# One Strassen level in the first product of an FFN beside a long convolution, PSUM seeded by ScalarE, and a second product in two-bank tiles

## The chip, the cores and the metric

The kernel runs on one core of one Trainium2 chip. The time is the device time of one execution in microseconds (us), the median over runs. The engines are named as in the profile: PE is the matrix engine, PEld its weight loads, DVE the vector engine, ACT the scalar engine, POOL the GpSimd engine, SP the queue that starts most DMAs.

## What is computed

The input x is 2048 tokens by 576 channels. After a layer norm two branches are added to x: a gated long convolution and a feed-forward network (FFN) with hidden width 4608.

```python
xn = layernorm(x)
# branch A: short conv over k, times v, long causal conv through an FFT, times xn
kv = shortconv(k, shift_k) * v
y  = irfft(rfft(kv, 2S) * rfft(ssm_k, 2S))[:S] + kv * ssm_D
a  = xn * y
# branch B
b  = relu(xn @ w1) @ w2          # w1 576x4608, w2 4608x576
return x + a + b
```

All arrays are float32. To keep that precision on PE, each operand is split into a high part and a low part (ACT copies the high part in a rounded format, DVE or POOL subtracts it from the source), and a product a·b is made of three matmuls: high·high, high·low, low·high.

## The kernel before

**The FFN.** The 4608 hidden columns are worked through in 12 chunks of 384 (`FT` = 3 tiles of 128), twice: the first pass for token blocks 0 and 1, the second for blocks 2 and 3 (512 tokens each). One turn is a chunk and a block. In it `mm1` makes three hidden tiles of 128 columns by 512 tokens: 14 matmuls of 512 columns each (L414: four chunks of 128 channels, three matmuls each, and the last 64 channels, where high and low part share one tile, with two). ACT writes relu of the result (`hh`, L420), DVE the rest (`ll`, L421). `mm2` multiplies the hidden tiles of the turn before with w2: for each of 4 tiles of 128 tokens and each half of 288 channels nine matmuls (L439), and DVE adds the result to the sum in SBUF (`acc`, L443, L449). PSUM has two banks for `mm1`, three for `mm2` and three for the convolution.

**The weights.** Each chunk's w1 and w2 are loaded raw by DMAs that POOL starts, ACT copies the high parts (L379, L388), and POOL subtracts (`split_lo`, L348). POOL reads two SBUF operands in each of these.

**The convolution** is a generator, `conv`, with four stages in this order: the filter's first transform (L474 to L482), the short convolution, gate and first transform of the data (L567 to L576, `tap`, `gate`, `stack`), the product in the frequency domain (L638 to L703), and the inverse transform with the output (L763 to L833). `tick` is called after every few matmuls of the FFN with their cost in PE columns. It lets the generator make at most one step at each call, and only while a balance that grows with the cost is not negative. So the convolution's instructions lie between those of the FFN in one fixed program order, and on each engine all of them run in that order. A step that waits holds up what stands behind it on its engine.

**The layer norm.** For the first block the rows are only centred before they are turned; the factor 1/std is applied where DVE adds `mm2`'s result (L443, one three-operand instruction). The other blocks are normalized beforehand.

Of the kernel before, what the change touches and what calls it, by code (L numbers as in the profile page):

```python
# [26 lines left out]
FT = 3  # L27
FC = FT * P
NCHUNK = DFF // FC
# [4 lines left out]
HT = T // HALVES  # L34

# [6 lines left out]
WARM_TILE = (0, 4, 0, 0)  # L42
LATE = (0, 1, 5)


W_MM1 = 14 * 512
W_MM2 = FT * 6 * NH
PAUSE = 16000
START = 4000
PAUSES = 17  # L50
# [9 lines left out]
FFT_TOTAL = N_FK * W_FK + N_FX * W_FX + N_FM * W_FM + N_FO * W_FO  # L60

SPLITS = {(0, 1): ((1, 0),), (0, 2): ((1, 1),), (1, 0): ((1, 2), (2, 0)), (1, 1): ((2, 1),),
          (1, 2): ((2, 2),)}
SPLITS0 = {(1, 0): ((1, 0), (1, 1)), (1, 1): ((1, 2), (2, 0)), (1, 2): ((2, 1), (2, 2))}
FFN_TOTAL = NCHUNK * NB * (FT * W_MM1 + BT * W_MM2)

# [46 lines left out]
def h3_ffn_kernel(ctx: ExitStack, tc, x, k, v, shift_k, ssm_k, ssm_D, w1, w2, fwd, inv, mid, out):  # L113
# [7 lines left out]
    wp = ctx.enter_context(tc.tile_pool(name="wp", bufs=2))  # L121
    hp = ctx.enter_context(tc.tile_pool(name="hp", bufs=2 * FT))
    xp = ctx.enter_context(tc.tile_pool(name="xp", bufs=2))
# [15 lines left out]
    rows_n = dram.tile([HB, BT // 2, 2, P, D], F32, name="rows_n")  # L139

# [33 lines left out]
    def load_x(t, tag, bufs, **queues):  # L174
        pair = xp.tile([P, 2, D], F32, tag=tag, name=f"{tag}{t}", bufs=bufs)
        move(pair, x, slice(t, t + 2), **queues)
        return pair

    def acc_pair(t, pair):
        pairs[t] = pair  # L180
        acc[t], acc[t + 1] = pair[:, 0, :], pair[:, 1, :]

    def load_acc(t, **queues):
        acc_pair(t, load_x(t, "acc", HT // 2, **queues))

    def add_x(t):

        for u in range(U):
            nc.gpsimd.dma_start(pairs[t][halves(u)[0]], x[u, :, t:t + 2], accum_op=OP.add)

    def stats(t, src):
        st = xp.tile([P, 2, 6], F32, tag="bn", name=f"bn{t}", bufs=4)
        for h in range(2):
            nc.vector.bn_stats(st[:, h, :], src[:, h * NH:(h + 1) * NH])
        nc.vector.bn_aggr(mv[:, t, :], st)

    def inv_std(t0, n):

        q = xp.tile([P, 3, 2 * BT], F32, tag="q", name=f"q{t0}")[:, :, :n]
# [8 lines left out]
    def normalized(dst, src, t):  # L208
        nc.vector.tensor_scalar(dst, src, mv[:, t, 0:1], rstd[:, t:t + 1],
                                op0=OP.subtract, op1=OP.mult)  # L210

    xT = {}
    done = {}

    def xT_tiles(b):
        hi = xp.tile([P, 4, 512], F32R, tag="xhi", name=f"xhi{b}")
        lo = xp.tile([P, 4, 512], F32R, tag="xlo", name=f"xlo{b}")
        hl = xp.tile([P, 512], F32R, tag="xhl", name=f"xhl{b}")
        xT[b] = (hi, lo, hl)

    def split_x(b, c, ps, cols=slice(0, 512)):
        hi, lo, hl = xT[b]
        if c < 4:
            high = nc.scalar.activation(hi[:, c, cols], ps[:, cols], AF.Copy)
            low = nc.vector.tensor_tensor(lo[:, c, cols], ps[:, cols], hi[:, c, cols],  # L225
                                          OP.subtract)
        else:
            high = done["act"] = nc.scalar.activation(hl[:64, cols], ps[:64, cols], AF.Copy)
            low = nc.vector.tensor_tensor(hl[64:, cols], ps[:64, cols], hl[:64, cols],
                                          OP.subtract)  # L230
        return high, low

    def centre(dst, src, t, how, behind=None):

        if how != "dve":
            neg = xp.tile([P, BT], F32, tag="neg", name=f"neg{t}", bufs=4)[:, :1]
        with tc.issue_after(behind.ins) if behind else nullcontext():
            if how == "act":  # L240
                nc.scalar.activation(dst, src, AF.Copy, scale=-1.0 / D, accum_out=neg)
            else:
                stats(t, src)
                if how == "dve":
                    return nc.vector.tensor_scalar(dst, src, mv[:, t, 0:1], None,
                                                   op0=OP.subtract)
                last = nc.vector.tensor_scalar(neg, mv[:, t, 0:1], -1.0, None, op0=OP.mult)
            act = nc.scalar.activation(dst, src, AF.Identity, bias=neg)
        return act if how == "act" else last

    def row_pairs(t0):
        pairs = [xp.tile([P, 2, D], F32, tag="xn", name=f"xn{t}", bufs=BT // 2)
                 for t in range(t0, t0 + BT, 2)]
        return [pairs[i // 2][:, i % 2, :] for i in range(BT)]
# [6 lines left out]
    def first_xT(srcs):  # L261

        xT_tiles(0)
        ps = []
        for c in range(5):
            ps.append(ps_o.tile([P, 512], F32, tag="o", name=f"psx{c}") if c >= 3 else fft_psum())
# [710 lines left out]
```

## Time and profile before

| | |
|---|---|
| median of 3 runs | 1071.23 us (1068.26 to 1071.31) |
| span of the profiled execution, first to last instruction | 1064.9 us |
| PE busy | 1055.7 us, 99% |
| PEld, DVE, ACT, POOL busy | 950.8, 747.9, 539.7, 408.8 us |
| granted PE clock | 1.00 in every 50 us but the last, 0.96 |
| the chain that ended last | PE 93%, DVE 5%, DMA 1% |

The profiled execution has no time of its own beside its span. The span is 6.3 us below the median of the runs. In a row of instructions the columns are: line, engine, operation, output <- inputs with their shapes, count | busy us, mean ns of one | idle time of the engine just before them and what ended it. A row of the timeline begins with its start and its duration. A row of the windows gives, for a stretch of the span, its length, and then PE, PEld, DVE, ACT and POOL busy in us, with the number of instructions; then the clock, the DMA share and GB/s.

### The profile page before, as it was taken

To read this page: it belongs to the slowest core of one execution; us is meant where nothing else is said; L and a number is where in the kernel's file an instruction comes from. 1 tells how busy PE (TensorE), PEld (TensorE's weight loads), DVE (VectorE), ACT (ScalarE), POOL (GpSimd) and SP (SyncE) were. 2 spreads that over 40 slices of the span, in tenths; PEclk is the share of its full clock that TensorE was granted. 3 is DMA by queue.
4 is the path that set the end of the run, shared out by engine and by line. 5 is a ranking of instruction groups with operands and counts; after the bars stand their busy time and mean duration, and the time that the engine had idled before them with its cause. 6 is when DMAs were issued, how large, how long until landed. Compare 5 with 4: busy or idle time off the path is not lost.

```text
span 1064.9 us, 17284 instructions
## 1 busy us (share of the span) xinstructions
PE 1055.7 (99%) x6228; PEld 950.8 (89%) x6228; DVE 747.9 (70%) x1207; ACT 539.7 (51%) x967; POOL 408.8 (38%) x465
## 2 busy tenths in 40 slices
PE   9999999999999999999999999999999999999998
PEld 6889999999998998999988888888888899999998
DVE  5322787858999788986557677766667737776774
ACT  5321787822433423424367777767776635443430
POOL 5261352423514424324425263424243364545520
PEclk9999999999999999999999999999999999999999
DMA  9990555674644448535566798667585679758624
GB/s 209 188 215 1 147 146 186 186 190 131 188 120 152 123 147 242 130 113 150 173 174 179 186 258 230 209 153 218 138 236 136 156 188 262 196 128 203 155 77 111
DMA packets 136785, 179.18 MB, mean 168 GB/s; under 512 B 69037, under 2 KB 73359, under 8 KB 136700
## 3 DMA queue, kind: packets, MB, share of 16 engines
q1 hardware_dynamic: 109756, 109.39, 38.5%
q0 software_dynamic: 26624, 67.95, 25.3%
q8 instruction: 49, 0.80, 0.3%
q10 hardware_dynamic: 320, 0.74, 0.3%
q14 instruction: 36, 0.29, 0.1%
HBM read 121.40 MB, written 42.47 MB: 154 GB/s over the span
## 4 chain that ended last, share of the span: by engine, by line
PE 93%; DVE 5%; DMA 1%; issue 0%; ACT 0%; SPq 0%
PE psh L414 41%; PE pso L439 41%; PE psf L647 6%; PE psf L481 3%; DVE e L570 1%; DVE c L571 1%; PE psf L830 1%; PE psf L831 1%; PE psf L700 1%; DVE xs L475 1%; DMA acc<-in_x 1%; DVE acc L443 0%; DVE c L567 0%; DVE acc L449 0%; DVE ll L421 0%
## 5 line engine op out<-in xcount | busy, mean ns | idle before, releaser
L348 POOL TENSOR_TENSOR l<-r,h 128x640 fp32r<-128x640 f32 (+1 forms) x144 | 229.7, 1613 | 316.8 <-ACT h L379 226.0
L439 PE MATMUL pso<-l,hh 128*128 128x288 f32 x1152 | 338.3, 295 | 0.0
L439 PE MATMUL pso<-h,hh 128*128 128x288 f32 x1152 | 336.2, 295 | 2.0 <-DVE acc L443 1.8
L439 PE MATMUL pso<-h,ll 128*128 128x288 f32 x1152 | 337.8, 295 | 0.0
L414 PE MATMUL psh<-xlo,h 128*128 128x512 f32 x576 | 226.4, 393 | 0.2 <-DVE xlo L225 0.2
L414 PE MATMUL psh<-xhi,h 128*128 128x512 f32 x576 | 225.5, 392 | 1.0 <-DVE ll L421 0.8
L439 PEld LDWEIGHTS pso<-h,hh 128*128 128x128 f32 x1152 | 215.3, 188 | 11.1 <-DVE acc L443 2.6
L414 PE MATMUL psh<-xhi,l 128*128 128x512 f32 x576 | 224.8, 391 | 0.0
L439 PEld LDWEIGHTS pso<-l,hh 128*128 128x128 f32 x1152 | 216.1, 188 | 7.6
L439 PEld LDWEIGHTS pso<-h,ll 128*128 128x128 f32 x1152 | 215.8, 188 | 1.7
L420 ACT ACTIVATE hh<-psh 128x512 fp32r<-128x512 f32 x144 | 85.6, 595 | 207.6 <-PE psh L414 204.8
L421 DVE SCALAR_TENSOR_TENSOR ll<-psh,hh 128x512 fp32r<-128x512 f32 x144 | 98.8, 687 | 110.2 <-ACT hh L420 109.4
L449 DVE TENSOR_TENSOR acc<-pso,acc 128x288 f32<-128x288 f32 x272 | 121.5, 451 | 63.3 <-PE pso L439 60.2
L414 PEld LDWEIGHTS psh<-xhi,l 128*128 128x128 f32 x576 | 108.2, 188 | 21.0
L414 PEld LDWEIGHTS psh<-xhi,h 128*128 128x128 f32 x576 | 108.1, 188 | 19.1 <-DVE ll L421 1.0
L414 PEld LDWEIGHTS psh<-xlo,h 128*128 128x128 f32 x576 | 108.1, 188 | 17.5 <-DVE xlo L225 0.8
L683 POOL DMA_DIRECT2D st<-yl x72 | 36.1, 533 | 106.6 <-PE psf L647 41.2
L443 DVE SCALAR_TENSOR_TENSOR acc<-pso,rstd,acc 128x288 f32<-128x288 f32 x96 | 48.1, 512 | 27.1 <-PE pso L439 26.5
L388 ACT ACTIVATE h<-r 128x576 fp32r<-128x576 f32 x72 | 48.4, 678 | 24.4 <-issue 13.2
L475 DVE TENSOR_TENSOR ks<-kt,ks 64x288 fp32r<-64x288 f32 x64 | 57.9, 905 | 3.9 <-ACT ks L474 1.9
L414 PE MATMUL psh<-xhl,h 128*128 128x512 f32 x144 | 56.3, 391 | 0.0
L414 PE MATMUL psh<-xhl,l 128*128 128x512 f32 x144 | 56.1, 390 | 0.0
(121 smaller groups left out, 1472.7 us busy)
## 6 DMA issues: line engine op xcount, KB each, us to landing
r<-in_w POOLq DMA_DIRECT2D x69, 288.0 KB, 5.5
r<-in_w POOLq DMA_DIRECT2D x23, 768.0 KB, 6.2
zk<-zk SPq DMA_DIRECT2D x32, 288.0 KB, 2.7
zx<-zx SPq DMA_DIRECT2D x32, 288.0 KB, 2.9
ztk<-zk SPq DMA_DIRECT2D x36, 256.0 KB, 4.0
ztx<-zx SPq DMA_DIRECT2D x36, 256.0 KB, 3.8
k<-k SPq DMA_DIRECT2D x72, 128.0 KB, 2.8
zo<-zy SPq DMA_DIRECT2D x32, 288.0 KB, 4.5
```

Of the source, the lines that this page charges most:

```text
L348: return nc.gpsimd.tensor_tensor(dst, src, hi, OP.subtract)
L388: nc.scalar.activation(h2, r2, AF.Copy)
L414: last = nc.tensor.matmul(ps, a, m, start=i == 0, stop=i == len(seq) - 1)
L420: done["act"] = nc.scalar.activation(hh, ps, AF.Relu)
L421: lows.append(nc.vector.scalar_tensor_tensor(ll, ps, 0.0, hh, op0=OP.max, op1=OP.subtract))
L439: nc.tensor.matmul(ps[:, :NH], a[:, cols], m[:, dc], start=n == 0, stop=n == 3 * FT - 1)
L443: done["acc"] = nc.vector.scalar_tensor_tensor(acc[t][:, dc], ps[:, :NH], rstd[:, t:t + 1], acc[t][:, dc], op0=OP.mult, op1=OP.add)
L449: done["acc"] = nc.vector.tensor_tensor(acc[t][:, dc], ps[:, :NH], acc[t][:, dc], OP.add)
L475: nc.vector.tensor_tensor(dst[other], src[own], dst[own], OP.subtract)
L481: nc.tensor.matmul(ps[:, :NH], w[:, u, n, :], stk, start=n == 0, stop=n == 1)
L647: nc.tensor.matmul(ps, a, m, start=n == 0, stop=n == 2)
L683: nc.gpsimd.dma_start(st[q * A2:(q + 1) * A2, i % GR, :], yl[i * A2:(i + 1) * A2, :])
```

## The change

The chunks become 256 columns wide (`FT` = 2), 18 for each half of the tokens. A chunk with two token blocks is a "quad", 36 in all. In a quad the four hidden tiles (2 of columns, 2 of tokens) times the four channel chunks form a two by two block product. Before it took eight products of 6 matmuls; now `quad` makes seven, by Strassen's scheme in Winograd's form, from sums of w1 blocks and of x blocks. The last 64 channels stay as they were (`rest`, 8 matmuls). Quad 0 is still made in the old way (`classical`). Everything else of the first product follows from that:

- The sums of w1 are made by POOL (`sums`, four more instructions per quad) and are split too, so that POOL splits 14 blocks of 128 by 128 per quad, and the last rows, where 256 columns had 8.
- The sums of x are made once by DVE; those of the second half are made during the first stage of the generator (`later_operands`, new), written to DRAM and loaded back when they are needed.
- The partial products are carried on in PSUM. ACT copies one bank to the next with the sign turned (`c`, `d`), or to SBUF (`u2`, `p5`), and DVE adds two of them.
- The second product has one tile of two banks (2 times 288 channels) per 128 tokens, two such tiles, and one DVE addition for both halves. Two of eight such units in a quad are "seeded": ACT copies the sum so far into PSUM, PE adds to it, and ACT copies it back, without DVE.
- PE's order in a quad is written out: a product, a unit of the second product (12 matmuls of 288 columns), a product, and so on. The convolution has two banks for three.
- `tick` is called 26 times per quad, with 1024, 1536 or 3456 columns. Before it was 14 times per turn, with 2592 or 3584. `START` and `PAUSES` differ.
- The first block is now normalized fully before it is turned, and 1/std is no longer applied later.

The diff, cut to its core:

```diff
-FT = 3
+FT = 2
-NCHUNK = DFF // FC
+NQ = DFF // FC
+QUADS = HALVES * NQ
-WARM_TILE = (0, 4, 0, 0)
+WARM_TILE = (0, 10, 0, 4)
+SEEDED = (1, 5)
-START = 4000
-PAUSES = 17
+START = 40000
+PAUSES = 19
-    ps_h = ctx.enter_context(tc.tile_pool(name="ps_h", bufs=2, space=PSUM))
-    ps_o = ctx.enter_context(tc.tile_pool(name="ps_o", bufs=3, space=PSUM))
-    ps_f = ctx.enter_context(tc.tile_pool(name="ps_f", bufs=3, space=PSUM))
+    ps_h = ctx.enter_context(tc.tile_pool(name="ps_h", bufs=1, space=PSUM))
+    ps_o = ctx.enter_context(tc.tile_pool(name="ps_o", bufs=2, space=PSUM))
+    ps_f = ctx.enter_context(tc.tile_pool(name="ps_f", bufs=2, space=PSUM))
...
+    def normalize_pair(xn, t):
+        for i in range(2):
+            stats(t + i, acc[t + i])
+        inv_std(t, 2)
+        normalized(xn[t % BT], acc[t], t)
+        return normalized_act(xn[t % BT + 1], acc[t + 1], t + 1)
...
+    def sums(g):
+        r1 = raw1[g]
+        t = sums_w[g] = wp.tile([P, 4, 2, P], F32, tag="sums", name=f"sums{g}")
+        w00, w01 = r1[:, 0:2, :P], r1[:, 0:2, P:]
+        w10, w11 = r1[:, 2:4, :P], r1[:, 2:4, P:]
+        for to, a, b in ((3, w00, w01), (0, t[:, 3], w11), (2, t[:, 0], w10), (1, w11, w01)):
+            nc.gpsimd.tensor_tensor(t[:, to], a, b, OP.add)
...
+    def product(ps, w, off, o, start=False):
+        for c in range(2):
+            h, l = w[:, 0, off + c, :], w[:, 1, off + c, :]
+            hi, lo = xo[o][:, 0, c, :], xo[o][:, 1, c, :]
+            matmuls(ps, ((h, hi), (h, lo), (l, hi)), start and c == 0)
+            tick(3 * W_MM)
...
+    def quad(g, units):
...
+        product(b, wa[g], 0, "00", start=True)
+        nc.scalar.activation(c, b, AF.Copy, scale=-1.0)
+        split_w2(g, 0)
+        unit(0)
+        product(b, wa[g], 2, "01")
+        rest(b, g, b0, 0)
+        hidden(g, 0, 0, b)
+        if more:
+            load_w2(g + 1, 0)
+            sums(g + 1)
+            split_a(g + 1)
+        unit(1)
+        product(c, wb[g], 0, "s2")
+        nc.scalar.activation(u2, c, AF.Copy)
+        split_w2(g, 1)
+        unit(2)
+        product(c, wb[g], 2, "s3")
+        nc.scalar.activation(d, c, AF.Copy, scale=-1.0)
+        if more:
+            split_b(g + 1)
+        unit(3)
+        product(d, wc[g], 0, "11")
+        rest(d, g, b1, 0)
+        hidden(g, 1, 0, d)
+        unit(4)
+        rest(c, g, b1, 1)
+        unit(5)
+        product(e, wc[g], 2, "s1", start=True)
+        nc.scalar.activation(p5, e, AF.Copy)
+        nc.vector.tensor_tensor(c, c, p5, OP.add)
+        hidden(g, 1, 1, c)
+        if more:
+            split_c(g + 1)
+        unit(6)
+        rest(e, g, b0, 1)
+        product(e, wd[g], 0, "s4")
+        nc.vector.tensor_tensor(e, e, u2, OP.add)
+        hidden(g, 0, 1, e)
+        if more:
+            split_d(g + 1)
+            split_r(g + 1)
+            if g + 2 < QUADS:
+                load_w1(g + 2)
+        unit(7)
...
+    def open_unit(g, b, i, n):
+        t = token(g, b, i)
+        ps = open_ps[g, t] = ps_o.tile([P, 2, 512], F32, tag="o", name=f"pso{g}_{t}")
+        if n in SEEDED and 0 < g < QUADS - 1:
+            seeded.add(t)
+            nc.scalar.activation(ps[:, :, :NH], two(acc[t]), AF.Copy)
...
+        if t in seeded:
+            done["act"] = nc.scalar.activation(two(acc[t]), ps[:, :, :NH], AF.Copy)
+            seeded.remove(t)
+        else:
+            done["acc"] = nc.vector.tensor_tensor(two(acc[t]), ps[:, :, :NH], two(acc[t]), OP.add)
+        tick(W_UNIT)
```

How the instructions move is shown at three places. The first is DVE in the short convolution, as one pass through four taps of a token tile. Before (`c`, `e`, `xs` are the convolution's sum, product and split; `acc` the second product's sum, `ll` a hidden tile's low part):

```order
L443 SCALAR_TENSOR_TENSOR acc_93<-pso_0_0_3084,rstd,acc_93 128x288
L443 SCALAR_TENSOR_TENSOR acc_93<-pso_0_1_3098,rstd,acc_93 128x288
L567 TENSOR_TENSOR c_3138<-k_3066,sk 128x576
L570 TENSOR_TENSOR e_1_3153<-k_2934,sk 128x576
L475 TENSOR_TENSOR xs_0_3095<-c_2992,xs_0_3095 64x576
L475 TENSOR_TENSOR xs_1_3113<-c_2992,xs_1_3113 64x576
L571 TENSOR_TENSOR c_3138<-c_3138,e_1_3153 128x576
L421 SCALAR_TENSOR_TENSOR ll_1_1_3157<-psh_1_1_3130,hh_1_1_3156 128x512
```

And now, in quad 13:

```order
L733 TENSOR_TENSOR e_1_3973<-k_3724,sk 128x576
L614 TENSOR_TENSOR acc_114<-pso_6_4262,acc_114 128x576
L734 TENSOR_TENSOR c_3932<-c_3932,e_1_3973 128x576
L634 TENSOR_TENSOR xs_0_3891<-c_3772,xs_0_3891 64x576
L634 TENSOR_TENSOR xs_1_3926<-c_3772,xs_1_3926 64x576
L733 TENSOR_TENSOR e_2_4005<-k_3595,sk 128x576
L614 TENSOR_TENSOR acc_114<-pso_7_4294,acc_114 128x576
L730 TENSOR_TENSOR c_4110<-k_4042,sk 128x576
L734 TENSOR_TENSOR c_3932<-c_3932,e_2_4005 128x576
L733 TENSOR_TENSOR e_3_4014<-k_3229,sk 128x576
L472 SCALAR_TENSOR_TENSOR ll_1_0_4362<-psh_4_4325,hh_1_0_4361 128x512
```

Of these eleven rows eight are the convolution's, of the eight before it was five; an `acc` row now covers both halves of the channels.

The second is POOL in the same stage. Before (`l` is a low part, `r` a raw weight, `wx` a transform matrix):

```order
L348 TENSOR_TENSOR l_7_0_2949<-r_7_2669,h_7_0_2948 128x640
L348 TENSOR_TENSOR l_7_1_3044<-r_7_2669,h_7_1_3043 128x640
L468 DMA wx_2940<-in_fwd 128x512
L348 TENSOR_TENSOR l_6_2_2815<-r_6_2_2413,h_6_2_2814 128x576
L370 DMA r_7_2_2818<-in_w 128x576
L348 TENSOR_TENSOR l_7_2_3117<-r_7_2669,h_7_2_3116 128x640
L348 TENSOR_TENSOR l_7_0_3125<-r_7_0_2677,h_7_0_3124 128x576
```

And now (`wa`, `wc`, `wd`, `wr`, `w` are the low parts of the blocks of w1 and of w2):

```order
L403 TENSOR_TENSOR wc_4122<-sums_3945,wc_4122 128x512
L627 DMA wx_3730<-in_fwd 128x512
L403 TENSOR_TENSOR wd_4161<-r_13_3874,wd_4161 128x256
L403 TENSOR_TENSOR wr_4164<-r_13_3874,wr_4164 128x256
L403 TENSOR_TENSOR w_4204<-r_13_0_3943,w_4204 128x576
L385 DMA r_14_4167<-in_w 128x4x256
L387 DMA r_14_4167<-in_w 64x256 x2
L395 DMA r_14_0_4252<-in_w 128x576
L414 TENSOR_TENSOR sums_4254<-r_14_4167 128x256 x2
L403 TENSOR_TENSOR w_4291<-r_13_1_4019,w_4291 128x576
L414 TENSOR_TENSOR sums_4254<-sums_4254,r_14_4167 128x256
L403 TENSOR_TENSOR wa_4259<-r_14_4167,wa_4259 128x512
```

The sums and the splits of the block sums have come in, and the raw w1 of the next quad is loaded only behind the last split of this one.

The third is ACT in the frequency-domain product. Before:

```order
L379 ACTIVATE h_17_1_8102<-r_17_7601 128x640
L726 ACTIVATE sw_8002<-psf 64x512
L727 ACTIVATE sw_8002<-psf 64x512
L638 ACTIVATE hix_8010<-ztx_7918 128x512
L688 ACTIVATE vo_8050<-psf 128x512
L688 ACTIVATE vo_8056<-psf 128x512
L675 ACTIVATE yh_8099<-k_20_7871 128x512
L388 ACTIVATE h_16_2_7817<-r_16_2_7219 128x576
```

And now, at the turn from quad 25 to 26 (`psh_2<-psh_1` is the copy from bank to bank with the sign turned):

```order
L471 ACTIVATE hh_0_1_8699<-psh_5_8611 128x512
L402 ACTIVATE wd_8703<-r_26_8277 128x256
L402 ACTIVATE wr_8706<-r_26_8277 128x256
L402 ACTIVATE w_8745<-r_26_0_8396 128x576
L851 ACTIVATE vo_8427<-psf 128x512
L851 ACTIVATE vo_8433<-psf 128x512
L838 ACTIVATE yh_8476<-k_18_8244 128x512
L514 ACTIVATE psh_2_8736<-psh_1_8735 128x512
L821 ACTIVATE k_20_8463<-psf 64x512
L821 ACTIVATE k_20_8466<-psf 64x512
```

The copy that PE waits for stands in one queue with the convolution's own rows and the splits, six of them since the last relu.

More of the change, by code (lines that the diff above doesn't have):

```diff
@@ L425, in mm2, with bank, matmuls @@
-    def mm2(ci, b, i):
-        t = b * BT + i
-        cols = slice(i * P, (i + 1) * P)
-        if ci == HALVES * NCHUNK - 1:
+    seeded = set()
+    banks = {}
+    def bank(g, which, name):
+        banks[g, name] = ps_h.tile([P, 512], F32, tag=f"h{(g + which) % 2}",
+                                   name=f"psh{g}_{name}")
+        return banks[g, name]
+    def matmuls(ps, seq, start):
+        for n, (a, m) in enumerate(seq):
+            with tc.issue_after(done["pe"].ins) if "pe" in done and not n else nullcontext():
+                last = nc.tensor.matmul(ps, a, m, start=start and n == 0, stop=n == len(seq) - 1,
+                                        skip_group_check=True)
+        done["pe"] = last
@@ L451, in mm2 @@
[L451 to L463 removed]
+            seq = []
@@ L880, in h3_ffn_kernel @@
     load_w1(0)
+    for t in range(BT, HT, 2):
+        load_acc(t)
     for j in range(FT):
```

621 lines of the change are left out of this document (330 added, 291 removed).

## The prediction

> **What bounds the kernel now.** I read the page first, then the windows of single stages, then the timeline where PE had lost time, then the groups of instructions. Two lines of the page:
>
> ```profile
> PE 1055.7 (99%) x6228; PEld 950.8 (89%) x6228; DVE 747.9 (70%) x1207; ACT 539.7 (51%) x967; POOL 408.8 (38%) x465
> PE 93%; DVE 5%; DMA 1%; issue 0%; ACT 0%; SPq 0%
> ```
>
> PE is busy nearly all the time and the chain that ended last runs along it. A busy share of matmuls can hide gaps, so I priced the matmuls from two stretches of the chain in order of time, of `mm1` and of `mm2`:
>
> ```profile
> 488.35 3.20 PE psh L414 x14
> ...
> 355.28 3.57 PE pso L439 x27
> ```
>
> A matmul of 512 columns takes 3.20/14 = 0.2286 us, one of 288 takes 3.57/27 = 0.132 us. The kernel before has 144 × 14 = 2016 of the first kind in `mm1` and 3456 of the second in `mm2`, together 461 + 457 = 918 us. The convolution's 306 long and 384 short ones (counted in its loops) make 121 us more. That leaves 26 us of the span for the first 13 us, the end and all stalls: a matmul taken away now is time taken away. The windows show one stretch in which PE lost something, beside one in which it did not:
>
> ```profile
> 250.00:350.00 100.00, 97.79 (x594) 89.03 (x594) 92.30 (x128) 35.77 (x69) 30.73 (x31) 1.00 0.49 146
> 550.00:850.00 300.00, 299.97 (x1675) 265.90 (x1674) 213.13 (x341) 217.98 (x379) 116.55 (x148) 1.00 0.71 190
> ```
>
> In the short convolution (250 to 350 us) DVE is busy 92% and PE loses 2.2 us. In the frequency-domain product ACT is busy 218 of 300 us and PE loses nothing. The timeline around 324 us shows how the 2.2 us were lost, in rows of DVE, POOL and PE:
>
> ```profile
> 323.85 3.93 DVE L570 TENSOR_TENSOR e<-k,sk 128x576 f32<-128x576 f32 x1
> 327.70 0.68 DVE L421 SCALAR_TENSOR_TENSOR ll<-psh,hh 128x512 fp32r<-128x512 f32 x1
> ...
> 324.19 2.96 POOL L348 TENSOR_TENSOR l<-r,h 128x640 fp32r<-128x640 f32 x2
> ...
> 328.43 0.50 PE L414 MATMUL psh<-xhi,h 128*128 128x512 f32 x1 [0.79 <-DVE ll L421]
> 330.58 0.41 PE L439 MATMUL pso<-h,hh 128*128 128x288 f32 x1 [1.42 <-DVE acc L443]
> ```
>
> Two POOL splits ran back to back, a DVE product of two SBUF operands took 3.93 us instead of its usual 0.75, `ll` and `acc` stood behind it, and PE waited 0.79 and 1.42 us. So DVE's queue, lengthened by POOL, is the next limit. The same stage's groups size it:
>
> ```profile
> L570 DVE TENSOR_TENSOR e<-k,sk 128x576 f32<-128x576 f32 x20 | 20.8, 1042 | 0.2
> L571 DVE TENSOR_TENSOR c<-c,e 128x576 f32<-128x576 f32 x23 | 19.1, 833 | 0.4
> L475 DVE TENSOR_TENSOR xs<-c,xs 64x576 fp32r<-64x576 f32 x14 | 12.9, 925 | 2.7 <-ACT xs L474 2.4
> L421 DVE SCALAR_TENSOR_TENSOR ll<-psh,hh 128x512 fp32r<-128x512 f32 x15 | 10.3, 685 | 1.8 <-ACT hh L420 1.7
> L449 DVE TENSOR_TENSOR acc<-pso,acc 128x288 f32<-128x288 f32 x18 | 8.1, 450 | 0.4 <-PE pso L439 0.2
> L567 DVE TENSOR_TENSOR c<-k,sk 128x576 f32<-128x576 f32 x7 | 7.4, 1060 | 0.0
> L576 DVE TENSOR_TENSOR c<-c,v 128x576 f32<-128x576 f32 x8 | 7.1, 891 | 0.1
> L348 POOL TENSOR_TENSOR l<-r,h 128x640 fp32r<-128x640 f32 (+1 forms) x12 | 20.1, 1682 | 25.2 <-ACT h L379 14.8 <-ACT h L388 10.4
> ```
>
> The rows with two SBUF inputs would take 0.75 us each unhindered, as this one did:
>
> ```profile
> 332.92 0.76 DVE L570 TENSOR_TENSOR e<-k,sk 128x576 f32<-128x576 f32 x1
> 333.59 0.68 DVE L421 SCALAR_TENSOR_TENSOR ll<-psh,hh 128x512 fp32r<-128x512 f32 x1
> 334.19 0.51 DVE L443 SCALAR_TENSOR_TENSOR acc<-pso,rstd,acc 128x288 f32<-128x288 f32 x1
> ```
>
> Their 72 rows sum to 67.3 us where 54 were due: 13 us lost in 20.1 us of POOL's splits, about 0.7 us for each us (with three rows on edge tiles left out). `ll` and `acc`, which read PSUM, stay at 685 and 450 ns.
>
> **The change, part by part.** The sum is made against the span, 1064.9 us; 6.3 us lie between it and the median of the runs, and I keep them.
>
> *Matmuls.* A quad has 50 of 512 columns for 4 × 14 = 56, in 35 of 36 quads. 210 × 0.2286 = 48.0 us go. `mm2` and the convolution keep theirs. Since PE is the limit nearly throughout, the whole of it would show, if PE stayed the limit: -48.
>
> *DVE at the start of the short convolution.* The stream makes at most one step per `tick`. The pauses in it leave a balance, and as long as that lasts, the stream runs at the rate of the ticks, now 26 in a quad's 24.1 us of FFN matmuls (50 × 0.2286 + 96 × 0.132) for 14 in 19.1 us. In DVE's queue the quads 12 to 14 hold 66 rows of 128x576 and 16 of 64x576 with two SBUF inputs, 18 `acc` rows of 576, and 18 of 512 on PSUM (12 `ll`, 6 additions of partial products). Start to start the three rows above take 0.67 and 0.60 us. An `acc` row of 576 is an estimate, 0.67, from 0.45 at 288 and 0.685 at 512. The `xs` rows I take at 0.78. That is 66 × 0.67 + 16 × 0.78 + 18 × 0.67 + 18 × 0.60 = 79.6 us, and PE's own matmuls there (150 long, 344 short) make 79.8. DVE is full before POOL costs it anything. POOL's elements per quad grow from 2432 (for 256 columns) to 4224, at 2.96/1280 us = 2.3 ns each, 2.4 by my estimate for the shorter instructions, 10.1 us a quad and 30.4 in three. At 0.7 us per us DVE needs 79.6 + 21.3 = 101, and PE waits about 21 us. In quads 15 to 18, DVE has 78.4 us by the same count and POOL 40.5, PE 104.9: 78.4 + 0.7 × 40.5 is 2 more than PE has. Quad 31, where the inverse transform starts, is priced by its own groups:
>
> ```profile
> L784 DVE TENSOR_TENSOR olo<-zo,ohi 128x576 fp32r<-128x576 f32 x32 | 29.0, 905 | 4.5 <-ACT ohi L783 2.5 <-DMA zo<-zl 1.9
> L833 DVE TENSOR_TENSOR y<-psf,low 64x288 f32<-64x288 f32 x64 | 28.5, 453 | 11.4 <-ACT low L832 10.5
> L792 DVE SCALAR_TENSOR_TENSOR y<-xt,mv,y 128x576 f32<-128x576 f32 x16 | 15.8, 985 | 0.0
> ```
>
> It holds 21 `y` rows of 64x288, 13 splits and 10 three-operand rows of 576 beside the FFN's 12. Unhindered, start to start, I take 0.38, 0.67 and 0.73 us (the means of the last two hold POOL's delays), and the sum is 31.6 us, with 10.1 of POOL against 28.1 of PE: 10.5. Together +34. With p us lost per us of POOL, the term is about 30p in quads 12 to 14 and 3.5 + 10p in quad 31. The Trainium skill ("SBUF — State Buffer", section "Who interferes with whom") has a rule that speaks against this change: a GpSimd instruction and a DVE instruction with two SBUF inputs exclude each other for the whole of the one that began first. The 3.93 us row and the PSUM rows at 685 and 450 ns agree with it. What it gives at its limit is the second rival.
>
> *The new handoffs.* In a quad PE now waits four times for an ACT copy out of PSUM or into it, and each has one unit of 12 × 0.132 = 1.58 us as cover. The copy is priced by the relu row, 0.6 us; ACT's queue decides. These rows carry that queue:
>
> ```profile
> 623.55 0.63 ACT L638 ACTIVATE hix<-ztx 128x512 fp32r<-128x512 f32 x1
> ...
> 629.62 0.70 ACT L388 ACTIVATE h<-r 128x576 fp32r<-128x576 f32 x1
> ...
> L474 ACT ACTIVATE ks<-kt 64x288 fp32r<-64x288 f32 x64 | 47.5, 742 | 4.5 <-DVE kt L514 3.1
> L482 ACT ACTIVATE zk<-psf 128x288 f32<-128x288 f32 x64 | 25.6, 403 | 13.8 <-PE psf L481 8.8 <-DMA zk<-zk 4.3
> L420 ACT ACTIVATE hh<-psh 128x512 fp32r<-128x512 f32 x36 | 21.3, 590 | 10.6 <-PE psh L414 10.5
> ```
>
> Back to back, the twelve instructions from 623.55 to 629.62 start 0.55 us apart. In the frequency-domain product (quads 21 to 29) a quad now has 57 ACT instructions, 21 of them new or the FFN's: 31.5 us, and PE has 31.9. In the filter's stage (quads 7 to 10) the sum of 15.5 `ks`, 14 `zk` and the FFN's 20 gives about 27.3 of 27.9. ACT is nearly full in 13 quads, a copy finds one or two rows ahead of it, and the cover holds about two. I take 1 us per quad, +13; the ends are 0 (cover holds) and 2 us per quad, +26.
>
> *The start.* These rows of before carry it, in DVE, ACT and PE:
>
> ```profile
> 8.91 0.82 DVE L194 BATCH_NORM_STATS2 bn<-acc 128x6 f32<-128x288 f32 x2 [1.09 <-DMA acc<-in_x]
> ...
> 24.38 0.16 DVE L201 TENSOR_SCALAR q<-mv 128x8 f32<-128x8 f32 x1
> ...
> 25.46 0.20 DVE L206 RECIPROCAL rstd<-q 128x8 f32<-128x8 f32 x1
> ...
> 12.14 0.50 PE L414 MATMUL psh<-xhi,h 128*128 128x512 f32 x1 [0.25 <-ACT xhi L224]
> ```
>
> Between the second pair's arrival at 8.9 and the first product at 12.1 us there now stand a second token's statistics (+1.0), the 1/std chain (25.66 - 24.38 = 1.3, and about 0.5 for a second crossing to ACT) and a longer row on ACT; with four weight splits ahead of a square root in ACT's queue I make that +4.5. Then the second block's statistics stand ahead of the first `ll` rows on DVE, and the operands of quad 1 come from a chain of ACT, DVE and POOL with no unit as cover. I estimate +6.5. Together +11, with ends 6 and 16.
>
> *The rest.* Seeding takes 68 of 288 additions off DVE, counted already. The raw w1 of the next quad now lands only after the last split of this one, and ACT's copy of it stands ahead of `u2`. In quads with little convolution I take 0.2 us each, +4, ends 0 and 10. Two banks for the convolution instead of three I price at nothing: DVE and ACT, which free them, are priced above. The end is the same: one addition and a store.
>
> Sum: 1064.9 - 48.0 + 34 + 13 + 11 + 4 = 1078.9 us of span, and with 6.3 about 1085 us.
>
> **The rivals.** *The other side: DVE keeps up.* The loss of 0.7 us per us of POOL is that of one stage, with POOL instructions of 1.4 to 1.7 us. Those of the change are shorter (256 to 576 columns), and each split waits for ACT, so DVE's rows may slip in between. For it speaks that in 550 to 850 us PE lost nothing. At 0.2 us per us the DVE term is 6 + 5.5 = 11.5 instead of 34, and the time 1085 - 22.5 = 1062.5 us, faster. The point that decides is 0.4 us per us: there the terms add up to 0. Against it speaks that at no loss at all quads 12 to 14 are level between DVE and PE.
>
> *POOL blocks in full.* If every POOL instruction in the crowded quads cost DVE its whole length, the DVE term would be 30.2 in quads 12 to 14, 78.4 + 40.5 - 104.9 = 14 in 15 to 18, and 31.6 + 10.1 - 28.1 = 13.6 in quad 31: 58 instead of 34, 1109 us. The quoted 0.7 of the fullest stage speaks against it. This is the limit of the Trainium skill's rule named above.
>
> **How the numbers follow.** The forecast has a chance of 0.45, DVE keeping up 0.38, full blocking 0.12; 0.05 is left for what I did not see. Less than 0.3%, about 3.2 us, can hardly be told from no change here. Faster than that by the sum needs less than 0.33 us per us (with the other terms as taken), slower more than 0.49. So I give 0.37 faster, 0.07 the same, 0.56 slower. The range: the first rival with the low ends of the start and the handoffs is below 1045, the second with the middle ones 1109, and with the high ends more. I leave out the far parts of both: 1042 to 1114 us.
>
> **What would show it.** Right: in the changed profile PE's windows show some 25 us lost over quads 12 to 14 (about 330 to 430 us) with `acc` and `ll` as releasers; the convolution's DVE rows mean over 1.0 us; POOL's busy time is over 500 us; the first product starts after 16 us; ACT is busy about 90% in quads 21 to 29. Wrong: a span under 1050 us with PE as full as now, or PE's waits mostly on ACT copies, which would make the handoffs, not DVE, the cost.

## The result, and the profile after

The changed kernel takes 1174.24 us (median of four runs, 1164.97 to 1176.21) against 1069.89 us (1068.26 to 1071.31) for the kernel before in the same runs: 1.0967 times as long, with a 95% interval of 1.0924 to 1.1011. The prediction was 1085 us, 1042 to 1114. The side was right, the size was not: 1174 lies 60 us outside. A run more than 1.5% above the fastest of its own kernel is left out of every comparison here; that leaves one run of four of late_wa and three of one_bank, both below. The profiled execution has a span of 1171.8 us. Three lines of its page, the engines' busy times and the slices of the granted clock and of PE:

```profile
PE 1062.8 (91%) x6028; PEld 932.2 (80%) x6028; DVE 839.0 (72%) x1154; ACT 730.9 (62%) x1358; POOL 629.6 (54%) x741
...
PE   7879899899997888899889999999999999789988
...
PEclk8989999899999999999889999999999999889999
```

The 200 fewer matmuls are there (210 less in the first product, ten more in the start's warm-up), but PE is no longer full, and the clock, which stood at 1.0 nearly throughout, now dips. To size it I priced every matmul by the prediction's 0.2286 us (512 columns) and 0.132 us (288) and summed what lies above that from one start to the next. Before, 10.7 us are lost so; after, 162.1, of which about 138 are waits and 24 matmuls that ran at half clock. The windows of the five stages of the changed kernel (start and the second half's operands; filter; short convolution; frequency-domain product; inverse transform) show where; the column behind the engines is the clock:

```profile
0.00:217.00 217.00, 189.02 (x1033) 159.29 (x1033) 124.55 (x226) 97.72 (x172) 109.95 (x129) 0.95 0.67 151
217.00:364.00 147.00, 137.79 (x829) 125.37 (x830) 97.30 (x123) 115.11 (x215) 73.73 (x89) 0.98 0.47 143
364.00:642.00 278.00, 246.77 (x1416) 219.82 (x1415) 226.82 (x268) 137.01 (x267) 151.31 (x159) 0.96 0.58 175
642.00:989.00 347.00, 334.61 (x1856) 289.88 (x1854) 243.82 (x344) 287.62 (x525) 197.22 (x246) 1.00 0.65 180
989.00:1171.80 182.80, 154.63 (x898) 137.83 (x898) 146.55 (x194) 93.42 (x182) 97.43 (x121) 0.94 0.65 165
```

PE lost in these stages, waits and half clock together, from one trace of each kernel (the columns behind the second are experiments told below):

| stage | before | after | pool_idle | wa_behind_u | wa_u_idle | eight_fine |
|---|---|---|---|---|---|---|
| start, operands | 4.9 | 43.7 | 34.1 | 42.0 | 31.7 | 35.6 |
| filter | 0.3 | 12.1 | 6.9 | 7.4 | 12.6 | 6.9 |
| short convolution | 3.2 | 48.6 | 27.3 | 34.6 | 18.2 | 10.3 |
| product | 1.7 | 21.9 | 13.1 | 19.3 | 15.9 | 20.3 |
| inverse | 0.6 | 35.9 | 33.6 | 31.0 | 20.4 | 24.4 |
| sum | 10.7 | 162.1 | 114.9 | 134.2 | 98.8 | 97.5 |

Three kinds of wait stand in the changed kernel's timeline. The first is the prediction's: POOL's instructions in a row hold up a DVE row with two SBUF inputs, and the second product's addition stands behind it and behind two more such rows (rows of DVE, POOL and PE alone, in order of time):

```profile
569.86 4.18 DVE L733 TENSOR_TENSOR e<-k,sk 128x576 f32<-128x576 f32 x1
570.02 1.44 POOL L414 TENSOR_TENSOR sums<-r 128x256 f32<-128x256 f32 x2
571.41 1.30 POOL L403 TENSOR_TENSOR wa<-r,wa 128x512 fp32r<-128x512 f32 x1
572.67 1.95 POOL L414 TENSOR_TENSOR sums<-sums,r 128x256 f32<-128x256 f32 x2
...
574.07 1.17 DVE L734 TENSOR_TENSOR c<-c,e 128x576 f32<-128x576 f32 x1
575.27 1.70 DVE L733 TENSOR_TENSOR e<-k,sk 128x576 f32<-128x576 f32 x1
576.89 0.74 DVE L614 TENSOR_TENSOR acc<-pso,acc 128x576 f32<-128x576 f32 x1
577.69 0.85 PE L451 MATMUL pso<-w,hh 128*128 128x288 f32 x2 [3.75 <-DVE acc L614]
```

The window behind that wait has the clock at 0.50:

```profile
577.60:583.40 5.80, 5.71 (x22) 5.52 (x23) 4.46 (x8) 1.36 (x2) 0.00 (x0) 0.50 0.87 248
```

In the second kind ACT stands at its copy of the next raw weights, whose DMA is late, and the copy `u` that PE needs stands behind it:

```profile
603.56 0.63 ACT L402 ACTIVATE wa<-r 128x512 fp32r<-128x512 f32 x1 [3.16 <-DMA r<-in_w]
604.09 0.58 ACT L531 ACTIVATE u<-psh 128x512 f32<-128x512 f32 x1
604.72 1.65 PE L451 MATMUL psh<-xs,wb 128*128 128x512 f32 x3 [2.99 <-ACT u L531]
```

The third is the same thing on DVE, with a load of the second half's rows ahead of `ll`:

```profile
72.70 0.82 DVE L186 BATCH_NORM_STATS2 bn<-xn 128x6 f32<-128x288 f32 x2 [3.78 <-DMA xn<-in_x]
73.44 0.68 DVE L472 SCALAR_TENSOR_TENSOR ll<-psh,hh 128x512 fp32r<-128x512 f32 x1
74.17 2.93 PE L451 MATMUL psh<-xs,wc 128*128 128x512 f32 x6 [7.40 <-DVE ll L472]
```

### The profile page after: what moved, and what is told of

Read it like the earlier page. It is cut to its first block, busy times and chain, and to the rows that moved or that the text cites. A ratio compares the mean times of both kernels' runs of the same rounds, so it can differ in the third digit from the quotient of the medians.

```text
span 1171.8 us, 17791 instructions
## 1 busy us (share of the span) xinstructions
PE 1062.8 (91%) x6028; PEld 932.2 (80%) x6028; DVE 839.0 (72%) x1154; ACT 730.9 (62%) x1358; POOL 629.6 (54%) x741
## 5 line engine op out<-in xcount | busy, mean ns | idle before, releaser
L451 PE MATMUL pso<-w,hh 128*128 128x288 f32 x2304 | 482.0, 299 | 18.4 <-DVE acc L614 18.4
L451 PEld LDWEIGHTS pso<-w,hh 128*128 128x128 f32 x2304 | 390.6, 191 | 49.0 <-DVE acc L614 27.8
L451 PE MATMUL pso<-w,ll 128*128 128x288 f32 x1152 | 343.3, 298 | 0.0
L614 DVE TENSOR_TENSOR acc<-pso,acc 128x576 f32<-128x576 f32 x220 | 165.6, 753 | 91.9 <-PE pso L451 90.3
L451 PEld LDWEIGHTS pso<-w,ll 128*128 128x128 f32 x1152 | 220.0, 191 | 1.5
L451 PE MATMUL psh<-xs,wb 128*128 128x512 f32 x420 | 116.1, 408 | 14.6 <-ACT u L531 14.4
L403 POOL TENSOR_TENSOR w<-r,w 128x576 fp32r<-128x576 f32 x72 | 109.9, 1527 | 16.4 <-ACT w L402 16.4
L451 PE MATMUL psh<-x,wa 128*128 128x512 f32 x420 | 110.6, 399 | 6.6 <-ACT psh L514 3.2
L451 PEld LDWEIGHTS psh<-xs,wb 128*128 128x128 f32 x420 | 77.5, 194 | 32.0 <-ACT u L531 19.2
L451 PE MATMUL psh<-hl,wr 128*128 128x512 f32 x280 | 89.6, 398 | 0.7 <-ACT p L558 0.7
```

What stands on the lines that cost most here:

```text
L403: nc.gpsimd.tensor_tensor(w[:, 1, :n], src, w[:, 0, :n], OP.subtract)
L451: last = nc.tensor.matmul(ps, a, m, start=start and n == 0, stop=n == len(seq) - 1, skip_group_check=True)
L614: done["acc"] = nc.vector.tensor_tensor(two(acc[t]), ps[:, :, :NH], two(acc[t]), OP.add)
```

## The experiments

All times are medians unless one run is named; ratios are to the kernel before in the same runs. Where no other kernel is named, the diff is against the changed kernel.

**Is it POOL?** *pool_idle* has nothing for POOL to compute:

```
-        nc.gpsimd.tensor_tensor(w[:, 1, :n], src, w[:, 0, :n], OP.subtract)
-            nc.gpsimd.tensor_tensor(t[:, to], a, b, OP.add)
```

> The changed kernel with nothing for POOL to compute: the low parts of the weights and the four sums of w1 are left out (the matmuls read the rounded weights twice, and raw blocks of w1 in place of the sums); every matmul, ACT and DVE instruction stays. If POOL's instructions, which hold up DVE's rows with two SBUF inputs, are the main cost (the prediction's theory), the 25 to 45 us of DVE waits in the short convolution and the inverse transform go, with about 15 us of half clock that follows them: 1105 to 1130 us, PE losing under 100 us for 162. Rival, waits for DMAs that stand in the queues of ACT and DVE ahead of what PE needs: those stay, over 1145 us.

Measured: 1127.42 us, 1.0528 (1.0478 to 1.0577): 47 us less than the changed kernel. The groups of DVE in the short convolution, first of the changed kernel, then of pool_idle, show what was taken away:

```profile
L734 DVE TENSOR_TENSOR c<-c,e 128x576 f32<-128x576 f32 x48 | 45.3, 944 | 0.7
L733 DVE TENSOR_TENSOR e<-k,sk 128x576 f32<-128x576 f32 x42 | 43.2, 1029 | 0.5
...
L634 DVE TENSOR_TENSOR xs<-c,xs 64x576 fp32r<-64x576 f32 x32 | 35.2, 1101 | 4.9 <-ACT xs L633 4.0
```

```profile
L739 DVE TENSOR_TENSOR c<-c,e 128x576 f32<-128x576 f32 x48 | 36.2, 753 | 0.7
L738 DVE TENSOR_TENSOR e<-k,sk 128x576 f32<-128x576 f32 x42 | 31.6, 752 | 0.4
...
L639 DVE TENSOR_TENSOR xs<-c,xs 64x576 fp32r<-64x576 f32 x32 | 24.1, 753 | 9.4 <-ACT xs L638 8.6
```

Without POOL each row takes 0.75 us. So POOL is a cause, but 60 us above the kernel before remain. PE still loses 114.9 us, not under 100, and the half clock did not go with POOL's waits: the mean granted clock is 0.968, for 0.969 in the changed kernel.

**Is it the seven products themselves?** *ffn_alone* ends the stream behind the second half's operands:

```
             yield from later_operands(fp)
+        return
```

> The changed kernel without the convolution: after the preparation of the second half's operands the stream ends, so that the seven products, their handoffs over ACT and DVE, the seeding and POOL's work run by themselves. PE has 35 quads of 24.1 us, one of 27.5 and about 20 us before the first product: 891 us. If the handoffs of the chain cost PE by themselves (1 us or more a quad), 930 us or more, with ACT's u and psh copies as releasers in every quad. If the losses come from the convolution's work in the same queues, under 910 us, the rest of it lost in the first 130 us.

Measured: 936.83 us. The windows of its first 150 us and of the next 750:

```profile
0.00:150.00 150.00, 126.73 (x646) 103.87 (x647) 96.61 (x189) 67.85 (x119) 70.75 (x85) 0.89 0.54 143
150.00:900.00 750.00, 749.56 (x4497) 677.67 (x4497) 268.97 (x375) 324.44 (x588) 419.37 (x487) 1.00 0.23 72
```

PE is busy 749.6 of 750 us: the chain of seven products, its copies over ACT and its seeds cost nothing by themselves. The time is above 910 us all the same, for the beginning loses more than the side of no cost had put there. *ffn_only* also leaves out the preparation of the second half's operands:

> ffn_alone (937 us) without the preparation of the second half's operands too (the second half takes the first's). ffn_alone lost 35 us of PE in its first 100 us. If that preparation, with its rows on DVE that wait for DMAs, is half of it, 912 to 922 us; if the start's own chain is nearly all of it, 930 us or more.

Measured: 922.33 us. About 15 us of the start are that preparation, which ran at 382 us in the kernel before and now runs from 56 us on. Without it 24 us are still lost in the first 150 us, where the kernel before loses 4: that is the start's own.

**Does order cost?** *late_wa* moves the sums and the copy of the next `wa` behind `u` in the code, and the next split, `split_b`, behind the fourth product:

```
-            sums(g + 1)
-            split_a(g + 1)
...
         nc.scalar.activation(u2, c, AF.Copy)
         split_w2(g, 1)
+        if more:
+            sums(g + 1)
+            split_a(g + 1)
...
-            split_b(g + 1)
...
         hidden(g, 1, 0, d)
+        if more:
+            split_b(g + 1)
```

> The changed kernel with one order changed: the sums and ACT's copy of the next quad's first weights are issued behind the copy u, and the next split behind the fourth product, so that no wait for the raw weights' DMA stands ahead of u in ACT's queue. If that in-order wait is what holds up u and the copy after it (27 us of PE's waits in 26 places, and about 5 us of half clock behind them), 1140 to 1155 us and the releaser u nearly gone. If ACT's queue is just full there, within 6 us of the changed kernel's 1174.

Measured: 1148.52 us, one run, so no verdict; it is 26 us below the changed kernel. It says little of the order, for in its trace the copy still stands ahead of `u` in 25 quads, for 26 in the changed kernel. What made this run shorter is not shown. *wa_behind_u* is late_wa with the order tied, since `split_a` is issued after `done["act"]`:

```
-        nc.scalar.activation(u2, c, AF.Copy)
+        done["act"] = nc.scalar.activation(u2, c, AF.Copy)
```

> late_wa once more, its order enforced: in late_wa the scheduler had put the copy that waits for the raw weights ahead of u in 25 of 35 quads again (26 in the changed kernel), so it tested little. Here the copy is issued after u in all 35. If this in-order wait holds PE up, the releasers u and the copy behind it (27 us in the changed kernel) shrink to a third and some 8 us of half clock go: 1140 to 1155 us. If not, 1165 us or more.

Measured: 1147.03 us, 1.0726 (1.0689 to 1.0763): 27 us less than the changed kernel, in the range that was expected of the in-order wait. In the waits of the changed kernel (waiter, releaser: us in total, times, longest) stand

```profile
ACT wa L402 <- DMA r<-in_w: 26.3, 22, 3.2
...
PEld psh L451 <- ACT u L531: 19.2, 18, 3.2
```

and in those of wa_behind_u PE's wait for `u` is gone but for 0.4 us; it is `u` that waits for PE:

```profile
ACT u L529 <- PE psh L451: 10.6, 20, 0.8
```

The 27 us are not all the order's. Priced as in the table, PE's waits for `u` cost 16 us in the changed kernel, and the edit also moves the sums and `split_b`. Three pairs of kernels told here differ by the tie alone: it is worth 11 us (pool_idle_late_wa to wa_u_idle), 8 us (splits_on_dve to wa_u_dve), and 1 us against late_wa's one run. So the order is a cause, of about 10 us; the rest of the 27 came with the moved splits and sums or lies in the spread of the runs, which stays open.

**Do the two add up?** *pool_idle_late_wa* was meant to tell, but late_wa's order did not hold there either (the copy stands ahead in 32 quads, in 31 of pool_idle).

> POOL's computing left out as in pool_idle (rounded weights read twice, raw blocks of w1 for the sums), and ACT's copy of the next first weights behind u as in late_wa. In pool_idle PE still lost 111 us, 25 of it waiting for u in 13 places, each with ACT standing up to 4.7 us at the copy that waits for the raw weights' DMA. If that in-order wait is a second cause beside POOL, the two add up: u's 25 us and some 8 us of half clock go, 1090 to 1102 us. If the wait only moves to another place behind the same DMA, over 1115 us.

Measured: 1119.41 us, 1.0473 (1.0426 to 1.0521). *wa_u_idle* is pool_idle with the order tied:

> wa_behind_u with POOL's computing left out as in pool_idle (1127 us; rounded weights read twice, raw blocks of w1 for the sums). If order and POOL add up, 1127 less 27 is 1100 us, 1092 to 1108, and u is hardly a releaser any more; if they were the same waits, 1118 us or more.

Measured: 1108.14 us, 1.0353 (1.032 to 1.0386): 66 us less than the changed kernel, where the two apart give 47 + 27. They nearly add up. 38 us above before remain, with the matmuls saved: 99 us are still lost.

**Can POOL's work go elsewhere?** *splits_on_dve* is late_wa with `nc.vector` for `nc.gpsimd` in both places, each row tied to its place in DVE's order (`here()`); *wa_u_dve* the same with the order of `wa` and `u` tied too.

> The changed kernel with late_wa's order and with all that POOL computes (the low parts of the weights, the sums) put on DVE. DVE gets 17 more rows a quad, by their sizes 5.6 us; POOL held up DVE by some 0.7 of its 10.1 us a quad, 7 us. If holding up is the cost, this is no worse than late_wa's 1167 us: 1140 to 1165. If DVE's own queue is the limit, with rows in it that wait for ACT and for DMAs, 1180 us or more.

Measured: 1141.89 us, 1.069 (1.0663 to 1.0717). The expectation compares with late_wa's 1167 us; against its one run of 1148.52 us this is 7 us less, too little to show anything against a single run.

> wa_behind_u (1147 us) with POOL's work on DVE as in splits_on_dve (1142 us, where late_wa, with the same code but for that, had 1167). The whole computation. If the two causes add up, 1115 to 1128 us; if they were the same waits, 1138 us or more.

Measured: 1134.21 us, 1.0607 (1.0585 to 1.063), the fastest of those that compute everything, and between the two ranges. The comparison that holds is with wa_behind_u: 13 us less, and every run of the one is below every run of the other. So with the order tied, POOL's work costs the kernel a little less on DVE than beside it.

**PSUM.** *before_two_banks* is the kernel before with one bank moved:

```
-    ps_o = ctx.enter_context(tc.tile_pool(name="ps_o", bufs=3, space=PSUM))
-    ps_f = ctx.enter_context(tc.tile_pool(name="ps_f", bufs=3, space=PSUM))
+    ps_o = ctx.enter_context(tc.tile_pool(name="ps_o", bufs=4, space=PSUM))
+    ps_f = ctx.enter_context(tc.tile_pool(name="ps_f", bufs=2, space=PSUM))
```

> The kernel before with two PSUM buffers for the convolution in place of three, and four for the second product in place of three: the one part of the change that the prediction priced at nothing. If it is worth nothing, within 3 us of before's 1068. If the convolution needs the third (in the changed kernel the inverse transform lost 36 us, most of it waiting for y, before 0.6), 1080 us or more, lost in the inverse transform.

Measured: 1102.32 us, 1.0316 (1.0295 to 1.0337): 34 us more. Its windows of the short convolution, of the inverse transform and of the end:

```profile
269.00:546.00 277.00, 266.43 (x1590) 242.47 (x1589) 236.93 (x366) 99.61 (x188) 93.65 (x91) 0.99 0.57 162
...
925.00:1087.00 162.00, 156.69 (x966) 143.42 (x966) 120.30 (x210) 67.97 (x132) 69.22 (x83) 1.00 0.68 175
1087.00:1100.80 13.80, 0.00 (x0) 0.00 (x0) 2.31 (x4) 0.40 (x1) 1.06 (x2) 0.55 0.22 60
```

PE is idle for some 16 us in the two stages, and the stream now ends behind the last matmul. So the loss is not in the inverse transform alone: priced as in the table it is some 7 us more than before at the start, 12 in the short convolution and 7 in the inverse transform, and the span ends 14 us behind the last matmul, for 4 before. *one_bank* gives the changed kernel its third buffer back, and pays with one-bank tiles of the second product (`ps_o` 3 x 1 bank, `ps_f` 3, additions and seeds of 288):

> The changed kernel with its second product in three one-bank tiles (two additions or seeds of 288 for one of 576), which gives the convolution its third PSUM buffer back. In the kernel before the third buffer was worth 34 us. If it is worth as much beside the seven products, 1135 to 1150 us, with the waits for y in the inverse transform (21 us) and at the taps' stage shorter. If the waits there come from what stands in the queues of DVE and ACT in any case, within 10 us of the changed kernel's 1174; DVE gets 35 us more to do (220 x 2 x 0.46 for 220 x 0.75), which could even cost.

Measured: 1175.91 us (three runs), 1.0987 (1.0934 to 1.1039): no gain. Its inverse transform lost 26.8 us for 35.9 and its short convolution 35.8 for 48.6, but its filter stage 23.8 for 12.1 and its product stage 27.3 for 21.9. *mended*, which adds this to wa_u_dve, agrees: it is slower than wa_u_dve.

> one_bank, wa_behind_u and splits_on_dve together, still the whole computation. If the causes add up (about 30 for POOL, 20 for the order, 30 for the bank), 1090 to 1110 us; seven products would then pay only if the start's 40 us went too. If DVE, with POOL's work and the shorter additions, is over-full in the short convolution, 1125 us or more.

Measured: 1151.77 us, 1.0791 (1.0736 to 1.0845). PE there waits some 30 us for the first copy of a quad, which stands on ACT behind seeds and splits, and once, for 9.6 us, behind a copy of the convolution that waits for a DMA.

**Longer pauses.** *patient*:

```
-                yield -PAUSE / 4
+                yield -PAUSE
...
-PAUSES = 19
+PAUSES = 25
```

> The changed kernel with longer pauses of the stream behind its loads (a full pause for each of the second half's pairs and operand blocks, one more ahead of the filter and of the taps; the rate is set for the rest). In the changed kernel PE waited 17 us in four places (to 74, 123, 219 and 370 us) because a DVE row that waits for a DMA stood ahead of one that PE needs, and about 10 us went in the half clock behind them. If so, those four go: 1145 to 1160 us. If the longer pauses only crowd the stream elsewhere, 1170 us or more.

Measured: 1178.71 us, 1.1007 (1.0967 to 1.1048). The beginning lost 32.4 us for 43.7, but the product stage 41.7 for 21.9: the waits moved.

**Eight products in the new layout.** *eight_products* and *eight_fine* call the eight-product form in every quad (no copies between products, no sums), with 16 and 28 turns of the stream.

> The changed kernel with eight products in place of seven: its tiles, two-bank second product, seeding, start and stream stay; the copies and additions between partial products and the sums of w1 are gone, POOL's elements go from 4224 to 2432 a quad, ticks from 26 to 16 a quad (the weights and operands taken are of the right sizes, not of the right blocks). 210 matmuls of 512 columns come back, +48 us. If the seven products' own instructions are the cost, 1075 to 1100 us. If the rest of the change (two-bank tiles, two PSUM buffers for the convolution, chunks of 256, the seeds) costs as much, over 1130 us.

Measured: 1169.12 us, 1.0934 (1.0904 to 1.0964).

> eight_products with a turn for the stream after every three matmuls (28 a quad), so that it no longer falls behind. PE has 1051 us of matmuls. If the layout (two-bank tiles, chunks of 256, two PSUM buffers for the convolution, the start) costs what eight_products lost outside its bad stretch, some 60 us, then about 1120 us, 1105 to 1130, and the seven products' own instructions cost the changed kernel about 100 us of waits for the 48 us of matmuls they save. If the layout is the whole cost, 1150 us or more; if it costs only the start's 25 us, under 1100.

Measured: 1156.87 us, 1.082 (1.0796 to 1.0845). By the time it is on the side of the layout as the whole cost. The turns were not the reason for the bad stretch that eight_products had; it is there again, with one wait of 19.3 us for a copy that waits for a DMA, placed ahead of the second product's matmuls. Its windows before, in and behind it:

```profile
150.00:950.00 800.00, 785.05 (x4573) 708.42 (x4573) 511.75 (x703) 490.25 (x909) 310.99 (x393) 0.99 0.63 171
950.00:1003.00 53.00, 25.80 (x114) 21.04 (x114) 23.13 (x38) 20.59 (x39) 18.77 (x25) 0.65 0.79 201
1003.00:1150.00 147.00, 140.55 (x859) 129.09 (x858) 105.52 (x157) 67.67 (x134) 65.63 (x86) 0.97 0.61 156
```

Of the 97 us lost, 33 fall between 950 and 1000. What holds in spite of that: with no seven products at all the layout loses some 60 us elsewhere, 36 of them before 212 us; and the short convolution, where the changed kernel lost 48.6 us, loses 10.3. So a loss of some 60 us, of the changed kernel's 162, is there in this layout without the seven products too.

**The clock.** *stalls* is ffn_alone with extra copies in place:

```
+        for _ in range(EXTRA[(g - 5) % len(EXTRA)] if g > 4 else 0):
+            nc.scalar.activation(d, d, AF.Copy)
```

> The changed kernel without the convolution (937 us), with 3 to 24 extra copies in place on ACT, 0.55 us each, in the chain between the third and the fourth product of one quad after the other: PE, which lost nothing there, is made to wait once a quad for about 1 to 12 us. This measures what a wait of a given length does to TensorE's clock. By the changed kernel's trace, where half clock followed waits of 2.1 to 7.6 us: waits under 2 us leave the clock at 1.0, over 4 us always bring a stretch at 0.5 of 3.4 us or more, and between it depends on the place. If the clock has to do with the work in the convolution and not with waits, no stretch of 0.5 follows here. The extra waits sum to about 140 us; with the clock's part, 1090 to 1130 us.

Measured: 1139.51 us (one run). The added waits sum to 165 us, the matmuls slowed by them to 39. By the length of PE's wait (33 of over 0.5 us, behind 110 us):

| wait | places | followed by clock 0.5 |
|---|---|---|
| 0.8 to 1.8 us | 7 | 0 |
| 2.1 to 3.3 us | 7 | 2 |
| 3.6 to 14.4 us | 19 | 19 |

PE's rows at one of 4.57 us, the first matmuls behind it slow, the last one at full speed:

```profile
494.42 2.93 PE L452 MATMUL psh<-x,wc 128*128 128x512 f32 x6 [4.41 <-ACT psh L541]
...
498.72 0.68 PE L452 MATMUL pso<-w,hh 128*128 128x288 f32 x2
...
499.38 0.42 PE L452 MATMUL pso<-w,hh 128*128 128x288 f32 x2
```

The window behind another wait of 4.57 us, which ended at 904.1:

```profile
904.10:908.90 4.80, 4.77 (x13) 4.00 (x14) 0.32 (x1) 0.60 (x1) 0.00 (x0) 0.50 0.01 3
```

So the waits together were paid again by about a quarter (39 of 165).

## Why the prediction was wrong in size

The four terms of loss gave 62 us; 151 more than before were lost (162.1 less 10.7). One step failed in most of them: beyond the start, a loss was priced only in quads where an engine's work comes near PE's or above it, and elsewhere put at nothing or 0.2 us. PE loses by single rows that stand in front of what it needs, in every stage.

*Matmuls, -48: right.* 210 are gone, 48.0 us at the prediction's price; with the ten more of the warm-up 46 us are gone in the trace. ffn_alone shows nothing lost to the chain.

*DVE held up by POOL, +34: the mechanism right, the sum short.* Quads 12 to 14 ran from 366 to 467 us, not from 330 to 430:

```profile
366.40:466.90 100.50, 85.75 (x494) 76.02 (x495) 97.62 (x116) 51.31 (x101) 56.17 (x56) 0.97 0.55 158
```

DVE is busy 97%, `acc` is what PE waits for most, and PE loses 20.7 us, where the prediction had 21. The same quads of pool_idle lose 9.9, so about half of it is POOL's. Elsewhere the term fails. Quads 15 to 18 lose 19.7 us, not 2 (pool_idle 12.6). Quad 31 loses 13.9, where it had 10.5, but pool_idle loses 14.1 there: POOL is not the cause, and the whole inverse transform loses 33.6 us without POOL's work and 35.9 with it. In sum, of the 47 us that pool_idle takes off, 21 are in the short convolution, 2 in the inverse transform, and 24 in the beginning, the filter and the product, where the prediction had POOL at nothing.

The rate was mis-sized too. Over the short convolution the five groups of rows with two SBUF inputs took 38 us longer than in pool_idle, 32 of them in the three groups shown, for 117 us of POOL (151 less 34): 0.33 us per us, not 0.7. Their means (0.93 to 1.10 us, for the over 1.0 named) are about what it said. With 0.33 in the prediction's own sum the DVE term is 17 us and the time 1068 us, no slower than before. That the side was right is therefore in part luck: it came from losses that were not in the sum.

*Handoffs over ACT, +13: the wrong step.* ACT's queue was priced by its fill. By itself the chain costs 0 (ffn_alone). What costs is, in part, one row of it that waits for a DMA ahead of `u`: PE waits 16 us for `u` in the changed kernel, and the tie alone is worth 8 to 11 us. The prediction saw that copy ("ACT's copy of it stands ahead of `u2`") and priced it at 0.2 us a quad, under "the rest".

*The start, +11: too small.* The first product starts at 18.9 us, as predicted (after 16), but 43.7 us are lost by 217 us, for 4.9 before. That the second half's operands are now prepared in the first quads, with DVE rows that wait for loads, was not counted; it is 15 us (ffn_alone less ffn_only). The start's own chain was mis-sized as well: without that preparation some 20 us more than before are lost in the first 150 us.

*Two PSUM buffers for the convolution, 0: not safe.* In the kernel before that alone costs 34 us. What it costs beside the seven products is not settled: one_bank gave it back and gained nothing, and whether its shorter rows took the gain is not shown.

*Not in the sum: the clock.* About 24 of the 162 us are matmuls at 0.5 behind waits. The prediction took the clock for 1.0, as it was before, where no wait was longer than 1.42 us in the rows it quoted. The Trainium skill ("TensorE: Matmul & The Clock Gate", "What's actually happening") has the rule: an idle window of about 3.4 us halves the clock. The stalls of 3.6 us and more agree, all 19; two of seven between 2.1 and 3.3 us were enough too, and there the measurement decides.

Of its signs, POOL over 500 us (629.6), the start, and the loss in quads 12 to 14 came; ACT was busy 83%, not 90%, in the product stage. PE's waits on ACT's copies (`u` 16 us, the copies from bank to bank some 13) do not outweigh those on DVE's rows (`acc` 21, `y` 21, `ll` 12), so its second sign of being wrong did not come. What the remaining 99 us of wa_u_idle are, one by one, stays open: 32 of them lie before 209 us, the rest follows DMAs that stand in front of PE's needs and single late rows, which were read from timelines and not taken away one by one.

## What to carry to other kernels

Ask of an edit not only how full it makes a queue, but which row in that in-order queue now waits for a DMA or a shared port ahead of a row that TensorE needs; taking one such row out of the way was worth about 10 us here, and moving it in the code alone did not move it in the queue (25 quads for 26). Work saved on the bounding engine counts only while that engine is kept full: in stalls 165 us of waits cost 39 us more through the clock. A kernel that loses 10 us in 1065 is balanced in everything at once, so a change of layout has to be priced by stage, the start and the buffers included, before its saving is believed.

## What the hardware showed

- TensorE's clock: in stalls half clock began 2.1 to 5.5 us after PE fell quiet and lasted 3.4 to 17.1 us, in steps of 3.4.
- One DVE row with two SBUF inputs can be held up by several POOL instructions in a row: 4.18 us against 0.75, with five instructions of POOL begun meanwhile, the first 0.16 us behind the start of the DVE row. The Trainium skill ("SBUF — State Buffer", "Who interferes with whom") has the exclusion for the whole of the instruction that was issued first; here, by the trace's starts, that would be DVE's, and it was held up through POOL's rows all the same (POOL's spans are rough).
- DVE rows that read PSUM were not held up: `acc` took 753 ns beside POOL's work and 755 without.
